# A grouped 1x1 convolution on one core: TensorE's unrolled program becomes a loop of 8 turns, and one ring becomes two

## The chip, the cores and the metric

The kernel runs on one NeuronCore of one Trainium2 chip. The metric is the device time of the whole program in microseconds (us); lower is better. The profile is of one execution on the chip.

## What is computed

The input x has 512 x 512 pixels of 192 channels, in bfloat16. The channels fall into 4 groups of 48, and each group is multiplied by its own 48 x 48 matrix. With k = 1 there is no padding, so it is one small matrix product per pixel and group:

```python
xg = x.reshape(1, 512, 512, 4, 48)
out = jnp.einsum('bhwgc,gcd->bhwgd', xg, w[0, 0])
return out.reshape(1, 512, 512, 192)
```

That is 262144 pixels of 384 B in and 384 B out, 201 MB in all.

## The kernel before

**Columns, groups, pairs, pieces.** The image is cut into pieces. A piece of `size` columns usually gives each of the 128 partitions of the on-chip memory `size` neighbouring pixels; a column is thus 128 pixels, one in each partition. Four columns are a *group*, two groups are a *pair*. `plan_pieces` lays the pieces out: a first slot in four small pieces (`HEAD`: 8, 20, 28 and 32 columns), then slots of `BIG` = 104 columns, and a last one of 48. There are 520 groups and 260 pairs.

**The ring.** All pieces live in one ring of 520 columns, five slots of 104. The results of a piece are written over its own input, and the piece is stored from there. So SyncE, which issues the loads (L217), waits in `wait_slot` until the piece five slots earlier has been stored. ScalarE issues the stores (L298).

**The work on a pair.** TensorE transposes the pair's pixels into `xT_ps` (L247, 12 transposes against an identity), VectorE copies them to one of three buffers `xT_sb` (L286, one copy a pair), TensorE multiplies them with block-shaped weights `wt` into `o_ps` (L262, 12 matmuls), and ScalarE copies each group's result from `o_ps` to the ring (L304, one copy a group). On TensorE the transposes of the next pair stand ahead of the matmuls of this one:

```python
for pair in range(NP):
    if pair + 1 < NP:
        transposes(pair + 1)
    matmuls(pair)
```

The semaphores `t_done`, `e_done`, `mm_done` and `fa_done` count pairs transposed, pairs copied by VectorE, groups multiplied and groups copied by ScalarE. All five engines' programs are written out in full: TensorE's has 3120 transposes, 3120 matmuls and as many weight loads.

**The shared piece.** One slot (`SHARED_AT`) is not spread over all 128 partitions. `SHARED` lists its blocks as (first row, rows, parts, columns, queue). A DMA whose outermost size is 4 is spread over four DMA engines, one whose outermost size is 11 over eleven. Before, two blocks of 16 rows and 72 columns go out in 4 parts from SyncE (and their stores from ScalarE), and one block of 44 rows and 64 columns in 11 parts from GpSimd. [...] Together the shares go to 15 of the 16 DMA engines; DMA engine 4 gets none.

**Stores at the end.** In the last slots (`LATE`) a piece is stored in two halves; a last piece of full size would be stored in four parts.

Of the kernel before, what the change touches and what calls it, by code (L numbers as in the profile page):

```python
# [12 lines left out]
UC = 2 * C  # L13
# [10 lines left out]

BIG = 104
RCOLS = 5 * BIG
HEAD = (8, 20, 28, 32)
LATE = 6
LATE_PARTS = (52, 52)
LAST_PARTS = (32, 32, 24, 16)  # L30
SHARED_AT = (9,)
SHARED_COLS = 72
SYNC, POOL = 0, 1
SHARED = ((0, 16, 4, SHARED_COLS, SYNC), (32, 16, 4, SHARED_COLS, SYNC), (52, 44, 11, 64, POOL))
CURSOR = 5
NXP = 4
NXS = 3
NOB = 4
# [21 lines left out]
class Piece:  # L60

    def __init__(self, i, slot, at, g0, size, shares, pix):
        self.i, self.slot, self.at, self.size = i, slot, at, size
        self.g0, self.g1 = g0, g0 + size // 4
        self.full = shares is None
        self.blocks = []
        for (r0, rows, parts, cols, queue) in shares or ((0, 128, 1, size, SYNC),):
            self.blocks.append(Block(r0, rows, parts, cols, queue, pix))
            pix += rows * cols
        self.pix_end = pix  # L70
        assert size % 4 == 0 and self.at + size <= RCOLS

# [4 lines left out]
def plan_pieces(npix):  # L77
    few = sum(rows * cols for _, rows, _, cols, _ in SHARED)
    at = list(SHARED_AT)
    if npix < len(at) * few + 128 * (sum(HEAD) + BIG * (at[-1] + 2)):  # L80
        at = []
    cols = (npix - few * len(at)) // 128
    assert cols % 4 == 0
    head = list(HEAD) if cols >= sum(HEAD) + BIG else []
    mid = cols - sum(head)
    slots = [[(BIG, None)]] * (mid // BIG) + ([[(mid % BIG, None)]] if mid % BIG else [])
    for i in at:
        slots.insert(i, [(SHARED_COLS, SHARED)])
    if head:
        slots.insert(0, [(s, None) for s in head])  # L90
    pieces, g, pix = [], 0, 0
    for n, parts in enumerate(slots):
        c = n * BIG % RCOLS
        for s, shares in parts:
            pieces.append(Piece(len(pieces), n, c, g, s, shares, pix))
            c, g, pix = c + s, pieces[-1].g1, pieces[-1].pix_end
    assert pix == npix
    return pieces


def bass_standalone__grouped__vision_kernel(nc, x, w, out):
# [7 lines left out]
    NG = pieces[-1].g1  # L109
    NP = (NG + 1) // 2  # L110

    xf = x.rearrange("b h w c -> (b h w) c")
# [17 lines left out]
    for p in pieces:  # L130
        late = pieces[-1].slot - p.slot
        parts = LAST_PARTS if late == 0 else LATE_PARTS if late < LATE else (BIG,)
        c = 0
        for n in parts if p.size == BIG and p.full else (p.size,):
            stores.append((p, c, c + n, p.g0 + (c + n) // 4))
            c += n
# [4 lines left out]
    with ExitStack() as es:  # L141
        block = es.enter_context(nc.Block())
        ring = es.enter_context(nc.sbuf_tensor("ring", [128, RCOLS * C], BF16))
        xT_sb = [es.enter_context(nc.sbuf_tensor(f"xT_sb{i}", [128, 4 * UC], BF16)) for i in range(NXS)]
# [14 lines left out]
        cur_sem = sem("cur_sem")  # L159
        cur = es.enter_context(nc.sbuf_tensor("cur", [CURSOR, 2 * len(pooled), 2, 32], BF16))  # L160
        w_sem, id_sem, e_sem, wb_sem, wc_sem = (sem(s) for s in ("w_sem", "id_sem", "e_sem", "wb_sem", "wc_sem"))
        p0_sem, p1_sem = sem("p0_sem"), sem("p1_sem")
        t_done, mm_done = sem("t_done"), sem("mm_done")
        e_done, fa_done = sem("e_done"), sem("fa_done")

        def columns(g):
            p = piece_of[g]
            at = p.at + 4 * (g - p.g0)
            return ring[:, at * C:(at + 4) * C]

        def wait_slot(wq, p):
            for q in pieces:
                if q.slot == p.slot - RCOLS // BIG:
                    wq.wait(st_sem[q.i], st_val[q])
                    if q in pl_sem:
                        wq.wait(ps_sem[q], pool_val[q])

        @block.gpsimd
        def _(gp):
# [12 lines left out]

            def pool_dmas(p, ap, inward, done):
                for dram, sbuf in transfers(ap, ring, p, POOL):
                    n = turns[0]
                    few = xf[0:CURSOR, 0:128].rearrange("p (a b) -> p a b", a=2)[:, :, 0:32]
                    gp.dma_start(cur[:, n], few).then_inc(cur_sem, 16)  # L197
                    turns[0] += 1
                    gp.dma_start(*((sbuf, dram) if inward else (dram, sbuf))).then_inc(done, 16)  # L199

            for p in pooled:
                wait_slot(wq, p)
                pool_dmas(p, xf, True, pl_sem[p])
                wq.wait(fa_done, p.g1)
                pool_dmas(p, of, False, ps_sem[p])
            for p in pooled:
# [3 lines left out]
        @block.sync  # L210
        def _(sp):
            wq = Waiter(sp)
            sp.dma_start(w_sb[:], wv).then_inc(w_sem, 16)  # L213
            for p in pieces:
                wait_slot(wq, p)
                for dram, sbuf in transfers(xf, ring, p, SYNC):
                    sp.dma_start(sbuf, dram).then_inc(ld_sem[p.i], 16)  # L217

        @block.tensor
        def _(pe):  # L220
            wq = Waiter(pe)

            def build_weights():
                wq.wait(e_sem, 1)
                wq.wait(w_sem, 16)
                last = None
# [6 lines left out]

            def transposes(pair):
                wq.wait(e_done, pair - 1)
                last = None
                for g in groups(pair):
                    p = piece_of[g]
                    if g == p.g0:
                        wq.wait(ld_sem[p.i], 16 * len(p.on(SYNC)))  # L240
                        if p in pl_sem:
                            wq.wait(pl_sem[p], pool_val[p])
                    xg = columns(g)
                    for ul in range(2):
                        for tc in range(3):
                            j = ul * 3 + tc
                            last = pe.transpose(xT_ps[:, g % NXP, j * 128:(j + 1) * 128],  # L247
                                                xg[:, j * 128:(j + 1) * 128], ident[:])
                last.then_inc(t_done, 1)

            def matmuls(pair):
                wq.wait(e_done, pair + 1)
                for g in groups(pair):
                    xs = xT_sb[pair % NXS][:, g % 2 * 2 * UC:(g % 2 + 1) * 2 * UC]
                    wq.wait(fa_done, g - 1)
                    last = None
                    for ul in range(2):
                        v = 2 * g + ul
                        for tc in range(3):
                            j = ul * 3 + tc  # L260
                            c0_, c1_ = COLR[tc]
                            last = pe.matmul(o_ps[:, v % NOB, c0_:c1_], lhsT=xs[:, j * 128:(j + 1) * 128],  # L262
                                             rhs=wt[:, WOFF[tc]:WOFF[tc] + (c1_ - c0_)],
                                             start=(tc == 0), stop=(tc == 2), skip_group_check=True)
                    last.then_inc(mm_done, 1)

            build_weights()
            wq.wait(id_sem, 1)
            transposes(0)
            wq.wait(wc_sem, 1)  # L270
            for pair in range(NP):
                if pair + 1 < NP:
                    transposes(pair + 1)
                matmuls(pair)

        @block.vector
        def _(dve):
# [3 lines left out]
            for pair in range(NP):  # L281
                n = len(groups(pair))
                b0 = pair * 2 % NXP
                wq.wait(t_done, pair + 1)
                wq.wait(mm_done, 2 * (pair - NXS + 1))
                dve.tensor_copy(xT_sb[pair % NXS][:, 0:n * 2 * UC].rearrange("p (g c) -> p g c", g=n),  # L286
                                xT_ps[:, b0:b0 + n, 0:2 * UC]).then_inc(e_done, 1)

        @block.scalar
        def _(act):  # L290
# [3 lines left out]
            def store():  # L294
                p, c0, c1, g1 = todo.pop(0)
                wq.wait(fa_done, g1)
                for dram, sbuf in transfers(of, ring, p, SYNC, c0, c1):
                    act.dma_start(dram, sbuf).then_inc(st_sem[p.i], 16)  # L298

            for g in range(NG):  # L300
                wq.wait(mm_done, g + 1)
                v = 2 * g
                dst = columns(g).rearrange("p (u c) -> p u c", u=2)
                act.copy(dst, o_ps[:, v % NOB:v % NOB + 2, 0:UC]).then_inc(fa_done, 1)  # L304
                while todo and todo[0][3] <= g:
                    store()
            while todo:
                store()
            for p in pieces:
# [29 lines left out]
```

## Time and profile before

| | us |
|---|---|
| median of 3 runs | 483.42 (482.58 to 484.23) |
| the profiled execution | 483.69 |
| its span, first to last instruction | 480.8 |
| around the span (the difference) | 2.9 |
| TensorE busy (matmuls and transposes) | 430.3 |
| ScalarE busy | 391.9 |
| VectorE busy | 249.6 |
| bytes moved by DMA, mean rate | 202.22 MB, 421 GB/s |

Read it with care for one thing: the share of an engine's busy time is a mean over the span, and a matmul's end is modelled, so a busy TensorE isn't one at its peak. The page has parts for busy time, the span in 40 slices, the DMA queues, the chain of work that ended last, the costliest groups of instructions and the DMA issues. Part 3 names the DMA queues by number: q1 carries SyncE's loads, q10 ScalarE's stores, q0 GpSimd's transfers, and q8 the code that TensorE runs. A group's row gives busy time and the mean duration of one instruction, then the engine's idle time ahead of them and what ended most of it. A row of the waits names who waited for whom, the total in us, how often, and the longest. The last compute instruction before begins near 460 us; the last store (2304 KB) is issued at 460.7 us and takes 19.7 us to land.

### The profile page before, as it was taken

What the parts mean: (1) busy time and instruction counts of PE and PEld (TensorE: products, weight loads), DVE (VectorE), ACT (ScalarE), POOL (GpSimd) and SP (SyncE); (2) the same over time, 40 slices, a digit from 0 to 9 for tenths busy, and PEclk for the clock granted to TensorE, in tenths of its full rate; (3) what the DMA queues carried; (4) which work ended last, traced back from release to release, by engine and by line L of the source; (5) the groups of instructions that cost most, each with busy time, mean ns of one, the idle gap of its engine ahead of it and who ended that gap; (6) DMA issues with size and microseconds to landing.
All of it is one profiled execution on the core that took longest, in us unless ns stands there. A gap on an engine that the chain in (4) does not pass through costs nothing.

```text
span 480.8 us, 13914 instructions
## 1 busy us (share of the span) xinstructions
PE 430.3 (89%) x6250; PEld 390.5 (81%) x6250; DVE 249.6 (52%) x261; ACT 391.9 (81%) x521; POOL 3.7 (1%) x12
## 2 busy tenths in 40 slices
PE   5979999999999999999679998989898999999910
PEld 5878898898898899889578887978787898898810
DVE  2535655655655655565335553545454556556500
ACT  2959999999998999899649995979797989999920
POOL 1000000000000001000000000000000000000000
PEclk9989999999999999999979998999999999999965
DMA  8999999999999999999999999999999999999995
GB/s 329 428 436 434 413 432 415 413 421 433 428 433 427 438 421 427 423 439 430 428 423 438 434 418 438 435 423 430 431 427 435 432 428 426 420 423 431 428 422 233
DMA packets 7913, 202.22 MB, mean 421 GB/s; under 512 B 1176, under 2 KB 1176, under 8 KB 1688
## 3 DMA queue, kind: packets, MB, share of 16 engines
q1 hardware_dynamic: 3560, 99.60, 48.5%
q10 hardware_dynamic: 4072, 99.58, 48.5%
q0 software_dynamic: 224, 2.16, 1.1%
q8 instruction: 49, 0.80, 0.6%
q14 instruction: 8, 0.07, 0.0%
HBM read 100.68 MB, written 100.66 MB: 419 GB/s over the span
## 4 chain that ended last, share of the span: by engine, by line
PE 47%; another core or an unknown queue 24%; DMA 23%; SPq 1%; issue 1%; ACT 0%
PE o_ps L262 27%; PE xT_ps L247 20%; DMA ring<-in_x_dram 13%; DMA out_dram<-ring 10%; SPq L217 1%; ACT ring L304 0%; SPq L213 0%; SPq L51 0%
## 5 line engine op out<-in xcount | busy, mean ns | idle before, releaser
L304 ACT CAST ring<-o_ps 128x768 bf16<-128x768 f32 x520 | 390.6, 802 | 68.0 <-PE o_ps L262 57.4
L286 DVE COPY xT_sb<-xT_ps 128x1536 bf16<-128x1536 bf16 x260 | 249.0, 958 | 205.1 <-PE xT_ps L247 205.1
L262 PE MATMUL o_ps<-wt,xT_sb 128*128 128x144 bf16 (+1 forms) x3120 | 290.6, 235 | 5.7 <-ACT ring L304 1.8
L262 PEld LDWEIGHTS o_ps<-wt,xT_sb 128*128 128x128 bf16 x3120 | 210.8, 98 | 43.1 <-ACT ring L304 32.8
L247 PE MATMUL xT_ps<-ident,ring 128*128 128x128 bf16 x3120 | 221.6, 222 | 20.9 <-DMA ring<-in_x_dram 20.5
L247 PEld LDWEIGHTS xT_ps<-ident,ring 128*128 128x128 bf16 x3120 | 190.8, 99 | 23.1 <-DMA ring<-in_x_dram 20.1
L197 POOL DMA_DIRECT2D cur<-in_x_dram x2 | 1.2, 622 | 242.7 <-DMA out_dram<-ring 188.8
L230 PE MATMUL o_ps<-w_sb,esel 48*128 48x48 bf16 x10 | 0.6, 209 | 2.8 <-DMA w_sb<-in_w_dram 2.8
L230 PEld LDWEIGHTS o_ps<-w_sb,esel 48*128 48x128 bf16 x10 | 0.4, 111 | 2.8 <-issue 2.8
L280 DVE CAST wt<-o_ps 128x480 bf16<-128x480 f32 x1 | 0.7, 658 | 3.4 <-PE o_ps L230 3.4
L304 ACT ACT_TABLE_LOAD x1 | 1.3, 1283 | 0.8 <-PEq L324 0.8
L199 POOL DMA_DIRECT2D ring<-in_x_dram x1 | 0.6, 563 | 0.0
L199 POOL DMA_DIRECT2D out_dram<-ring x1 | 0.6, 559 | 0.0
L184 POOL TENSOR_SCALAR_AFFINE_SELECT esel<-esel 48x272 bf16<-48x272 bf16 x1 | 0.4, 402 | 0.0
L181 POOL MEMSET esel<- 48x272 bf16 x1 | 0.3, 317 | 0.3 <-POOLq L324 0.3
L188 POOL TENSOR_SCALAR_AFFINE_SELECT ident<-ident 128x128 bf16<-128x128 bf16 x1 | 0.3, 282 | 0.0
L182 POOL MEMSET ident<- 128x128 bf16 x1 | 0.2, 198 | 0.0
L324 POOL MEMSET const-bfloat16-1.0<- 128x1 bf16 x1 | 0.1, 101 | 0.0
L324 POOL MEMSET const-uint8-127<- 128x1 uint8 x1 | 0.1, 101 | 0.0
L324 POOL MEMSET const-float32-0.0<- 128x1 f32 x1 | 0.1, 98 | 0.3 <-issue 0.3
L324 POOL MEMSET const-float32-1.0<- 128x1 f32 x1 | 0.1, 98 | 0.0
## 6 DMA issues: line engine op xcount, KB each, us to landing
ring<-in_x_dram SPq DMA_DIRECT2D x18, 4992.0 KB, 33.4
out_dram<-ring ACTq DMA_DIRECT2D x13, 4992.0 KB, 51.4
out_dram<-ring ACTq DMA_DIRECT2D x10, 2496.0 KB, 43.5
ring<-in_x_dram SPq DMA_DIRECT2D x1, 2304.0 KB, 16.3
out_dram<-ring ACTq DMA_DIRECT2D x1, 2304.0 KB, 19.7
ring<-in_x_dram SPq DMA_DIRECT2D x1, 1536.0 KB, 11.1
out_dram<-ring ACTq DMA_DIRECT2D x1, 1536.0 KB, 40.8
ring<-in_x_dram SPq DMA_DIRECT2D x1, 1344.0 KB, 7.9
```

What stands on the lines that cost most here:

```text
L181: gp.memset(esel[:], 1.0).then_inc(p0_sem, 1)
L184: gp.affine_select(out=esel[:], in_=esel[:], pattern=[[-1, ECOLS]], compare_op=AluOpType.is_equal, fill=0.0, base=ESHIFT, channel_multipli ...
L197: gp.dma_start(cur[:, n], few).then_inc(cur_sem, 16)
L199: gp.dma_start(*((sbuf, dram) if inward else (dram, sbuf))).then_inc(done, 16)
L217: sp.dma_start(sbuf, dram).then_inc(ld_sem[p.i], 16)
L230: last = pe.matmul(o_ps[:, NOB - 1, col:col + CG], lhsT=esel[:, s0:s0 + 128], rhs=w_sb[:, g, :], start=True, stop=True, skip_group_check=True)
L247: last = pe.transpose(xT_ps[:, g % NXP, j * 128:(j + 1) * 128], xg[:, j * 128:(j + 1) * 128], ident[:])
L262: last = pe.matmul(o_ps[:, v % NOB, c0_:c1_], lhsT=xs[:, j * 128:(j + 1) * 128], rhs=wt[:, WOFF[tc]:WOFF[tc] + (c1_ - c0_)], start=(tc == ...
L280: dve.tensor_copy(wt[:], o_ps[:, NOB - 1, 0:WCOLS]).then_inc(wc_sem, 1)
L286: dve.tensor_copy(xT_sb[pair % NXS][:, 0:n * 2 * UC].rearrange("p (g c) -> p g c", g=n), xT_ps[:, b0:b0 + n, 0:2 * UC]).then_inc(e_done, 1)
L304: act.copy(dst, o_ps[:, v % NOB:v % NOB + 2, 0:UC]).then_inc(fa_done, 1)
L324: nc = _bacc.Bacc("TRN2", target_bir_lowering=False, num_devices=1)
```

## The change

- **Loop.** TensorE's program is one pair of transposes, then a loop of 8 turns (`pe.Fori`). A turn does 32 pairs, 64 groups (`LOOP`), and at its end subtracts what the turn used from three semaphores, so that each turn can wait for the same constants. The matmuls of the last group stand behind the loop.
- **Two rings.** `xin` and `xout` have 256 columns each, three slots of 88, 84 and 84. A loop turn goes round them once. A load waits for the transposes (`t_done`) of the pieces that lay there before; ScalarE waits for the store of what lay in `xout` before it writes.
- **Landings through GpSimd.** TensorE no longer waits for a piece's own load semaphore. GpSimd waits for each load in turn and adds the piece's pairs to `ready`; TensorE waits for `ready` at the places in a turn where some piece begins (`starts`).
- **Shared piece.** Now 32 rows in 4 parts from SyncE and 88 rows in 11 parts from GpSimd, all of 64 columns: 120 rows, 8 for each of 15 DMA engines. It stands in slot 12, with a piece of 24 columns behind it in the same slot. In all there are 513 groups.
- **Buffers and waits.** `xT_sb` has two buffers instead of three, and some waits that the order on TensorE implies are gone. A store is issued one group later, without a wait for ScalarE's own copy.
- **Stores at the end.** The pieces of the last slots go out in halves, the last full one in parts of 24, 20, 20 and 20, and the last piece has 4 columns.

The diff, cut to its core:

```diff
-BIG = 104
-RCOLS = 5 * BIG
+RING = 256
+SLOTS = (88, 84, 84)
 HEAD = (8, 20, 28, 32)
 LATE = 6
-LATE_PARTS = (52, 52)
-LAST_PARTS = (32, 32, 24, 16)
-SHARED_AT = (9,)
-SHARED_COLS = 72
+LAST_PARTS = (24, 20, 20, 20)
+LOOP = RING // 4
+SHARED_AT = (12,)
+SHARED_COLS = 64
 SYNC, POOL = 0, 1
-SHARED = ((0, 16, 4, SHARED_COLS, SYNC), (32, 16, 4, SHARED_COLS, SYNC), (52, 44, 11, 64, POOL))
+SHARED = ((0, 32, 4, 64, SYNC), (32, 88, 11, 64, POOL))
 CURSOR = 5
 NXP = 4
-NXS = 3
+NXS = 2
 NOB = 4
...
-    pieces, g, pix = [], 0, 0
-    for n, parts in enumerate(slots):
-        c = n * BIG % RCOLS
+    pieces, g, pix, n = [], 0, 0, 0
+    while cols:
+        size = SLOTS[n % len(SLOTS)]
+        c = sum(SLOTS[:n % len(SLOTS)])
+        parts = [(s, None) for s in HEAD] if n == 0 and cols >= size else []
+        if n in at:
+            parts = [(SHARED_COLS, SHARED)]
+        left = size - sum(s for s, _ in parts)
+        if min(left, cols):
+            parts.append((min(left, cols), None))
         for s, shares in parts:
             pieces.append(Piece(len(pieces), n, c, g, s, shares, pix))
+            cols -= 0 if shares else s
             c, g, pix = c + s, pieces[-1].g1, pieces[-1].pix_end
+        n += 1
     assert pix == npix
     return pieces
...
+    LP = LOOP // 2
+    turns_of_loop = max(NP - 1, 0) // LP
+    starts = sorted({p.g0 // 2 % LP for p in pieces})
...
-        parts = LAST_PARTS if late == 0 else LATE_PARTS if late < LATE else (BIG,)
+        half = p.size // 8 * 4
+        parts = (p.size,)
+        if p.full and p.size in SLOTS and late < LATE:
+            parts = LAST_PARTS if late == 1 and p.size == sum(LAST_PARTS) else (p.size - half, half)
         c = 0
-        for n in parts if p.size == BIG and p.full else (p.size,):
+        for n in parts:
...
-        ring = es.enter_context(nc.sbuf_tensor("ring", [128, RCOLS * C], BF16))
+        xin = es.enter_context(nc.sbuf_tensor("xin", [128, RING * C], BF16))
+        xout = es.enter_context(nc.sbuf_tensor("xout", [128, RING * C], BF16))
...
-        def columns(g):
-            p = piece_of[g]
-            at = p.at + 4 * (g - p.g0)
-            return ring[:, at * C:(at + 4) * C]
-
-        def wait_slot(wq, p):
-            for q in pieces:
-                if q.slot == p.slot - RCOLS // BIG:
-                    wq.wait(st_sem[q.i], st_val[q])
-                    if q in pl_sem:
-                        wq.wait(ps_sem[q], pool_val[q])
+        ready, e_left, o_left = sem("ready"), sem("e_left"), sem("o_left")
+
+        def columns(ring, g):
+            c = g % LOOP * 4
+            return ring[:, c * C:(c + 4) * C]
+
+        def before(p):
+            return [q for q in pieces if q.g0 < p.g0 - LOOP + p.size // 4 and q.g1 > p.g0 - LOOP]
...
-            for p in pooled:
-                wait_slot(wq, p)
-                pool_dmas(p, xf, True, pl_sem[p])
-                wq.wait(fa_done, p.g1)
-                pool_dmas(p, of, False, ps_sem[p])
+            for p in pieces:
+                ahead = pieces[p.i + 1] if p.i + 1 < len(pieces) else None
+                if ahead in pooled:
+                    wq.wait(t_done, max([(q.g1 + 1) // 2 for q in before(ahead)], default=0))
+                    pool_dmas(ahead, xf, xin, True, pl_sem[ahead])
+                wq.wait(ld_sem[p.i], 16 * len(p.on(SYNC)))
+                if p in pooled:
+                    wq.wait(pl_sem[p], pool_val[p])
+                pairs = (NP if p is pieces[-1] else p.g1 // 2) - p.g0 // 2
+                if pairs:
+                    gp.sem_inc(ready, pairs)
+                if p.i and pieces[p.i - 1] in pooled:
+                    q = pieces[p.i - 1]
+                    wq.wait(mm_done, q.g1 + 2)
+                    pool_dmas(q, of, xout, False, ps_sem[q])
...
-                wait_slot(wq, p)
-                for dram, sbuf in transfers(xf, ring, p, SYNC):
+                wq.wait(t_done, max([(q.g1 + 1) // 2 for q in before(p)], default=0))
+                for dram, sbuf in transfers(xf, xin, p, SYNC):
                     sp.dma_start(sbuf, dram).then_inc(ld_sem[p.i], 16)
...
-            def transposes(pair):
-                wq.wait(e_done, pair - 1)
+            def transposes(j, gs):
+                if j % LP in starts:
+                    n = min((s - j) % LP or LP for s in starts)
+                    pe.wait_ge(ready, min(j + n, NP - first[0]))
...
-                for g in groups(pair):
-                    p = piece_of[g]
-                    if g == p.g0:
-                        wq.wait(ld_sem[p.i], 16 * len(p.on(SYNC)))
-                        if p in pl_sem:
-                            wq.wait(pl_sem[p], pool_val[p])
-                    xg = columns(g)
+                for g in gs:
+                    xg = columns(xin, g)
...
-            def matmuls(pair):
-                wq.wait(e_done, pair + 1)
-                for g in groups(pair):
-                    xs = xT_sb[pair % NXS][:, g % 2 * 2 * UC:(g % 2 + 1) * 2 * UC]
-                    wq.wait(fa_done, g - 1)
+            def matmuls(j, gs):
+                pe.wait_ge(e_left, j + 1)
+                for g in gs:
+                    xs = xT_sb[j % NXS][:, g % 2 * 2 * UC:(g % 2 + 1) * 2 * UC]
+                    pe.wait_ge(o_left, g + 1)
...
+            first = [0]
             build_weights()
-            wq.wait(id_sem, 1)
-            transposes(0)
-            wq.wait(wc_sem, 1)
-            for pair in range(NP):
-                if pair + 1 < NP:
-                    transposes(pair + 1)
-                matmuls(pair)
+            pe.wait_ge(id_sem, 1)
+            pe.sem_inc(o_left, 2)
+            transposes(0, groups(0))
+            pe.wait_ge(wc_sem, 1)
+            if turns_of_loop:
+                with pe.Fori(0, turns_of_loop):
+                    for j in range(LP):
+                        transposes(j + 1, range(2 * j + 2, 2 * j + 4))
+                        matmuls(j, range(2 * j, 2 * j + 2))
+                    pe.sem_inc(ready, -LP)
+                    pe.sem_inc(e_left, -LP)
+                    pe.sem_inc(o_left, -LOOP)
+            first[0] = LP * turns_of_loop
+            for j in range(NP - first[0]):
+                g0 = 2 * first[0]
+                if j + 1 < NP - first[0]:
+                    transposes(j + 1, [g - g0 for g in groups(first[0] + j + 1)])
+                matmuls(j, [g - g0 for g in groups(first[0] + j)])
...
-                wq.wait(mm_done, 2 * (pair - NXS + 1))
                 dve.tensor_copy(xT_sb[pair % NXS][:, 0:n * 2 * UC].rearrange("p (g c) -> p g c", g=n),
-                                xT_ps[:, b0:b0 + n, 0:2 * UC]).then_inc(e_done, 1)
+                                xT_ps[:, b0:b0 + n, 0:2 * UC]).then_inc(e_left, 1)
...
-                wq.wait(fa_done, g1)
-                for dram, sbuf in transfers(of, ring, p, SYNC, c0, c1):
+                for dram, sbuf in transfers(of, xout, p, SYNC, c0, c1):
                     act.dma_start(dram, sbuf).then_inc(st_sem[p.i], 16)
...
             for g in range(NG):
+                p = piece_of[g]
+                if g == p.g0:
+                    for q in before(p):
+                        wq.wait(st_sem[q.i], st_val[q])
+                        if q in pooled:
+                            wq.wait(ps_sem[q], pool_val[q])
...
-                dst = columns(g).rearrange("p (u c) -> p u c", u=2)
-                act.copy(dst, o_ps[:, v % NOB:v % NOB + 2, 0:UC]).then_inc(fa_done, 1)
-                while todo and todo[0][3] <= g:
+                dst = columns(xout, g).rearrange("p (u c) -> p u c", u=2)
+                act.copy(dst, o_ps[:, v % NOB:v % NOB + 2, 0:UC]).then_inc(o_left, 1)
+                while todo and todo[0][3] < g:
                     store()
             while todo:
+                act.wait_ge(o_left, todo[0][3] - LOOP * turns_of_loop + 2)
                 store()
```

More of the change, by code (lines that the diff above doesn't have):

```diff
@@ L70, in __init__ @@
         self.pix_end = pix
-        assert size % 4 == 0 and self.at + size <= RCOLS
+        assert size % 4 == 0 and self.at + size <= RING
     def on(self, queue):
@@ L79, in plan_pieces @@
     at = list(SHARED_AT)
-    if npix < len(at) * few + 128 * (sum(HEAD) + BIG * (at[-1] + 2)):
+    if npix < len(at) * few + 128 * RING * (2 + at[-1] // len(SLOTS)):
         at = []
@@ L83, in plan_pieces @@
     assert cols % 4 == 0
[L84 to L90, printed above, removed]
-    pieces, g, pix = [], 0, 0
-    for n, parts in enumerate(slots):
-        c = n * BIG % RCOLS
+    pieces, g, pix, n = [], 0, 0, 0
[8 more added lines that the diff above has]
+            parts.append((min(left, cols), None))
         for s, shares in parts:
             pieces.append(Piece(len(pieces), n, c, g, s, shares, pix))
+            cols -= 0 if shares else s
             c, g, pix = c + s, pieces[-1].g1, pieces[-1].pix_end
+        n += 1
     assert pix == npix
@@ L159, in bass_standalone__grouped__vision_kernel @@
         cur_sem = sem("cur_sem")
-        cur = es.enter_context(nc.sbuf_tensor("cur", [CURSOR, 2 * len(pooled), 2, 32], BF16))
+        cur = es.enter_context(nc.sbuf_tensor("cur", [CURSOR, 2 * max(len(pooled), 1), 2, 32], BF16))
         w_sem, id_sem, e_sem, wb_sem, wc_sem = (sem(s) for s in ("w_sem", "id_sem", "e_sem", "wb_sem", "wc_sem"))
@@ L163, in bass_standalone__grouped__vision_kernel @@
         t_done, mm_done = sem("t_done"), sem("mm_done")
-        e_done, fa_done = sem("e_done"), sem("fa_done")
-        def columns(g):
-            p = piece_of[g]
-            at = p.at + 4 * (g - p.g0)
-            return ring[:, at * C:(at + 4) * C]
-        def wait_slot(wq, p):
-            for q in pieces:
-                if q.slot == p.slot - RCOLS // BIG:
-                    wq.wait(st_sem[q.i], st_val[q])
-                    if q in pl_sem:
-                        wq.wait(ps_sem[q], pool_val[q])
+        ready, e_left, o_left = sem("ready"), sem("e_left"), sem("o_left")
[4 more added lines that the diff above has]
+            return [q for q in pieces if q.g0 < p.g0 - LOOP + p.size // 4 and q.g1 > p.g0 - LOOP]
         @block.gpsimd
@@ L191, in _, with pool_dmas @@
             turns = [0]
-            def pool_dmas(p, ap, inward, done):
+            def pool_dmas(p, ap, ring, inward, done):
                 for dram, sbuf in transfers(ap, ring, p, POOL):
@@ L220, in _ @@
         def _(pe):
-            wq = Waiter(pe)
             def build_weights():
-                wq.wait(e_sem, 1)
-                wq.wait(w_sem, 16)
+                pe.wait_ge(e_sem, 1)
+                pe.wait_ge(w_sem, 16)
                 last = None
@@ L232, in build_weights @@
                 last.then_inc(wb_sem, 1)
-            def transposes(pair):
-                wq.wait(e_done, pair - 1)
+            def transposes(j, gs):
+                if j % LP in starts:
+                    n = min((s - j) % LP or LP for s in starts)
+                    pe.wait_ge(ready, min(j + n, NP - first[0]))
                 last = None
-                for g in groups(pair):
-                    p = piece_of[g]
-                    if g == p.g0:
-                        wq.wait(ld_sem[p.i], 16 * len(p.on(SYNC)))
-                        if p in pl_sem:
-                            wq.wait(pl_sem[p], pool_val[p])
-                    xg = columns(g)
+                for g in gs:
+                    xg = columns(xin, g)
                     for ul in range(2):
                         for tc in range(3):
-                            j = ul * 3 + tc
-                            last = pe.transpose(xT_ps[:, g % NXP, j * 128:(j + 1) * 128],
-                                                xg[:, j * 128:(j + 1) * 128], ident[:])
+                            i = ul * 3 + tc
+                            last = pe.transpose(xT_ps[:, g % NXP, i * 128:(i + 1) * 128],
+                                                xg[:, i * 128:(i + 1) * 128], ident[:])
                 last.then_inc(t_done, 1)
-            def matmuls(pair):
-                wq.wait(e_done, pair + 1)
-                for g in groups(pair):
-                    xs = xT_sb[pair % NXS][:, g % 2 * 2 * UC:(g % 2 + 1) * 2 * UC]
-                    wq.wait(fa_done, g - 1)
+            def matmuls(j, gs):
[3 more added lines that the diff above has]
+                    pe.wait_ge(o_left, g + 1)
                     last = None
@@ L259, in matmuls @@
                         for tc in range(3):
-                            j = ul * 3 + tc
+                            i = ul * 3 + tc
                             c0_, c1_ = COLR[tc]
-                            last = pe.matmul(o_ps[:, v % NOB, c0_:c1_], lhsT=xs[:, j * 128:(j + 1) * 128],
+                            last = pe.matmul(o_ps[:, v % NOB, c0_:c1_], lhsT=xs[:, i * 128:(i + 1) * 128],
                                              rhs=wt[:, WOFF[tc]:WOFF[tc] + (c1_ - c0_)],
```

## The prediction

> **What bounds the kernel now.** I read the page's slices first, then its DMA queues, then busy time by stretches of the span (short ones at the end), then the waits.
>
> The page, parts 1 and 2 (busy time of each engine; the forty slices):
>
> ```profile
> PE 430.3 (89%) x6250; PEld 390.5 (81%) x6250; DVE 249.6 (52%) x261; ACT 391.9 (81%) x521; POOL 3.7 (1%) x12
> ...
> DMA  8999999999999999999999999999999999999995
> GB/s 329 428 436 434 413 432 415 413 421 433 428 433 427 438 421 427 423 439 430 428 423 438 434 418 438 435 423 430 431 427 435 432 428 426 420 423 431 428 422 233
> ```
>
> TensorE looks fuller than ScalarE, but only the DMA row is at 9 from the second slice to the last but one. The page's part 3 says what fills it:
>
> ```profile
> q1 hardware_dynamic: 3560, 99.60, 48.5%
> q10 hardware_dynamic: 4072, 99.58, 48.5%
> q0 software_dynamic: 224, 2.16, 1.1%
> q8 instruction: 49, 0.80, 0.6%
> ```
>
> Loads, stores, GpSimd's transfers and TensorE's code together are 98.7% of what 16 DMA engines had in the span. The stretches (us, then busy us and count by engine, granted clock, DMA share, GB/s) show where the rest is:
>
> ```profile
> 444.00:456.00 12.00, 11.85 (x178) 10.69 (x176) 7.24 (x8) 10.94 (x16) 0.00 (x0) 1.00 1.01 427
> 456.00:468.00 12.00, 3.19 (x42) 2.51 (x40) 1.38 (x2) 4.38 (x6) 0.00 (x0) 0.72 1.00 430
> 468.00:472.00 4.00, 0.00 (x0) 0.00 (x0) 0.00 (x0) 0.00 (x0) 0.00 (x0) 0.50 0.84 361
> 472.00:476.00 4.00, 0.00 (x0) 0.00 (x0) 0.00 (x0) 0.00 (x0) 0.00 (x0) 0.50 0.79 339
> 476.00:480.80 4.80, 0.00 (x0) 0.00 (x0) 0.00 (x0) 0.00 (x0) 0.00 (x0) 0.50 0.14 61
> ```
>
> No engine computes after 461 us; the end is DMA alone. The share falls in steps: at 0.79 of 16, about three DMA engines have finished, the others near 476, and a few run to 480. So the time is the longest of sixteen nearly full DMA engines. Compute only has to keep them fed, and does:
>
> ```profile
> ACT ring L304 <- PE o_ps L262: 57.4, 119, 7.2
> ...
> PEld o_ps L262 <- ACT ring L304: 32.8, 142, 1.5
> PE xT_ps L247 <- DMA ring<-in_x_dram: 20.5, 9, 5.7
> ```
>
> TensorE waits for loads nine times, and ScalarE then for TensorE. Between such waits ScalarE's copies set the pace:
>
> ```profile
> L304 ACT CAST ring<-o_ps 128x768 bf16<-128x768 f32 x520 | 390.6, 802 | 68.0 <-PE o_ps L262 57.4
> ```
>
> In the timeline at 160 us five copies take 4.07 us, 0.815 us a group.
>
> **Sixteen chains.** The trace lists every DMA packet with start and duration. Under load a packet starts 3 ns before another ends, so the packets can be strung into 16 chains, one per DMA engine. A load packet of 39936 B takes 1.476 us (27.06 B/ns), one of 27648 B 1.025 us, one of 24576 B 0.912 us. The shared pieces' packets label the chains:
> - Four carry 16 packets of 27648 B (16.4 us), the SYNC share. They end at 476.9, 477.3, 480.0 and 480.0.
> - Eight carry 8 of 24576 B (7.3 us), the POOL share, and all code pages between them, six or seven each. They end at 475.8 to 477.7, mean 476.5.
> - Three carry the POOL share and no pages: 468.0 to 468.7, mean 468.4. So six pages cost 8.1 us, some 1.3 us each: a page packet takes 1.0 us and the data packet behind it about 1.85 instead of 1.476.
> - One carries neither, yet ends at 476.2: its store packets take about 1.58 us all through. It is DMA engine 4, left out now as after.
>
> **The change, part by part.**
>
> *Shares.* A shared piece holds 7680 pixels instead of 5120, so whole rows give each DMA engine (262144-7680)/16 = 15904 pixels, 160 fewer. A pixel is 768 B in and out, so that is 123 KB, 4.5 us less for all sixteen. The share becomes 8 rows of 64 columns in and out, 16 packets of 0.912 us, 14.6 us, for all but engine 4.
>
> *Code.* The loop body is 768 matmuls with their weight loads plus 37 waits, semaphore steps and the branch: 1573 instructions, 6.1 pages of 256; TensorE's whole program is 6.4 pages where it was 49.9. If the body stays in TensorE's instruction store, pages fall from 49 to at most 7. No trace here has a backward branch, so the bounds are 0 and 49 pages saved, or even some lost. I take saved: successive pages go to the eight DMA engines in a fixed turn, every eighth to the same one, which looks like eight slots, and 6.1 pages plus one ahead fit in eight. Against it: the first page is fetched at 16.1 us, when 281 instructions have run, so a page is asked for as soon as one is left; if that overwrites the page just left, the loop's head is gone before the first branch back.
>
> [...]
>
> *Sum by chain,* with the body held:
> - SYNC four: -4.5-16.4+14.6 = -6.3, so 470.6 to 473.7.
> - Eight with pages: -4.5-7.3+14.6-8.1 = -5.3, mean 471.2.
> - Three without: -4.5-7.3+14.6 = +2.8, mean 471.2.
> - Engine 4: -4.5, 471.7.
>
> The last chain ends at 473.7. From the last packet to the span's end were 0.8 us (480.8-480.0), from span to the profiled execution's time 2.9 (483.69-480.8): 477.4 us. That execution stands 0.27 us over the median of 483.42. The seven first pages fall on chains with 2.5 us to spare.
>
> *Branches back.* Seven are taken. Each costs TensorE three semaphore steps, an addition and the branch; at the 0.24 us of the shortest waits in the timeline, about a microsecond, 7 us in all, hidden as below. With a missing page: 1.0 us for the page, up to two packets of 1.476 ahead of it, 4 us.
>
> *Ring.* 520 columns shared in place become 256 in and 256 out. A load now waits for the transposes of the slot three back, not for a store five slots back (before, SP waited 342.9 us in 15 waits for stores). ScalarE waits for the store three slots back, and behind it on ScalarE are only later copies and their stores. A column is 49152 B each way, 0.114 us at 430 GB/s, so a slot of 84 costs DMA 19.2 us and compute 21 x 0.815 = 17.1. Compute is the faster, so when it frees a slot the DMA still has work: cost nothing. If that cover goes, a refill starts on an empty queue; the smallest load (384 KB, 0.9 us of transfer) landed in 3.3, so 2.4 us are lost each time. There are 513 groups instead of 520, 5.7 us less for ScalarE, so compute needs 418 us. At the start 256 columns keep the DMA busy until about 31 us; the first slot of 22 groups is through by about 26 (ScalarE did 20 copies in the first 24 us): no gap, but the margin is small.
>
> *GpSimd* now passes each landing on to TensorE by `ready`. Queued behind its waits are its own two shared transfers; the pooled store waits for two further groups of a six-group piece, so the next slot's `ready` is not late. A relay is priced at the 0.3 us that GpSimd's first wait in the waits' view lasts, at most 37 of them, 11 us of compute spread over the span; but the next loads are queued by then, so the DMA loses nothing.
>
> *Smaller edits.* Two xT_sb buffers, dropped waits that the order of TensorE implies, stores issued one group later, a tail in parts down to 4 columns: nothing, since DMA has a backlog to the end.
>
> **The rivals.**
>
> *Code is fetched again each turn (slower).* Then 8 turns of 7 pages are 56, seven on each of the eight chains: 471.2+9.3 = 480.5, plus 0.8 and 2.9 is 484.2. Stalls of 4 us are covered by three slots a turn at 19.2-17.1 = 2.1 us each, 6.3, with little left, so I add 0 to 6 us: 484 to 490, middle 487. If pages past the loop's end come in as well and are thrown away, up to eight a turn, 9 us more: 496. It decides from the point where the body and what is fetched ahead exceed the store. For it speaks the eager first fetch, against it the turn of eight. [...] Chance 0.22.
>
> *The smaller ring starves the DMA (about level).* Two or three empty starts of 2.4 us at the beginning and at branches undo the gain: 480 to 485. The 33 us in which a load now lands (in the median) speak for it; the 2.1 us of compute in hand per slot against. Chance 0.10.
>
> *The rotation stops but the longest chain doesn't shorten (the change doesn't do what it says).* If the SYNC share is not on the four chains I think, the last chain stays at 480 less 4.5, 479 us in all. The landing of each share four by four speaks against. Chance 0.05, inside the range.
>
> **Numbers.** Body held: 0.63, 475 to 480, likeliest 477.4. Chains as long as now but for the 4.5 us: 0.05, 479. Refetch 0.22, 487. Starved 0.10, 482.5, of it 0.02 faster, 0.05 the same, 0.03 slower. A measurement of this kernel can tell 0.3%, 1.5 us. So faster 0.70, same 0.05, slower 0.25. The range goes from 474.5 (all chains level at 471, less a microsecond) to 488.5, past the middle of the refetch case.
>
> **What would show it.** Held: queue q8 with about 7 packets, DMA share near 1.00 until 470, then a fall within 3 us. Refetched: 56 packets or more, TensorE waiting some 4 us every 64 groups, and a DMA tail with seven or eight engines late. Starved: DMA slices under 9 in mid-span. The prediction is wrong if q8 stays above 49 packets, or if any mid-span slice falls below 400 GB/s.

## The result, and the profile after

| | before | after |
|---|---|---|
| median, four runs each on one chip, us | 483.81 (482.58 to 484.23) | 488.89 (488.58 to 489.35) |
| profiled execution, us | 483.69 | 489.35 |
| its span, us | 480.8 | 487.6 |

The changed kernel takes 1.0117 times as long (95% interval 1.0102 to 1.0132): 5.1 us slower by the medians (5.7 by the ratio), where the prediction had 6.0 us faster.

The forty slices and the queues of the page of after:

```profile
DMA  8999999999999999999999999999999999999976
GB/s 310 432 411 434 429 433 421 431 429 431 431 439 432 431 432 434 400 331 388 434 429 442 405 392 428 414 418 437 426 427 429 436 428 437 427 428 423 430 293 269
...
q1 hardware_dynamic: 4276, 98.52, 47.9%
q10 hardware_dynamic: 5076, 98.50, 47.5%
q0 software_dynamic: 352, 4.33, 2.6%
q8 instruction: 6, 0.10, 0.1%
```

Three things are to be seen.

**The code stays.** q8 has 6 packets where it had 49. They come at 19.3, 28.5, 38.2, 45.7, 54.6 and 61.8 us, all in the first of eight turns (the second begins at 64.3 us).

**The DMA engines are busy and move less.** The DMA row stands at 9 through the middle of the span, yet the row under it falls to 331 and 388 GB/s in the slices from 207 to 232 us, and again to 392 near 286. Those are the load and the store of the shared piece. Two stretches of after (us, then busy us and count by engine, granted clock, DMA share, GB/s) show it closer:

```profile
204.00:216.00 12.00, 11.89 (x182) 10.93 (x180) 6.70 (x7) 10.99 (x15) 0.00 (x0) 1.00 0.99 340
216.00:228.00 12.00, 8.90 (x113) 8.26 (x111) 4.27 (x5) 6.95 (x11) 0.00 (x0) 0.86 1.03 357
```

The share is 0.99 and more at 340 to 357 GB/s, where before moved 427 in a full stretch. The busy share alone doesn't tell this loss; bytes have to be read beside it. In the packet list, packets of 24576 B, 0.912 us each before, now take 1.153 us in the mean on GpSimd's queue (the longest 2.644), 1.207 among SyncE's loads and 1.022 among the stores of the same rows.

**The end is ragged.** Stretches of the end of after:

```profile
464.00:468.00 4.00, 3.92 (x59) 3.43 (x57) 2.65 (x3) 3.68 (x6) 0.00 (x0) 1.00 0.44 187
...
472.00:476.00 4.00, 3.96 (x61) 3.59 (x59) 2.53 (x3) 3.52 (x6) 0.00 (x0) 1.00 0.79 328
476.00:480.00 4.00, 3.96 (x64) 3.67 (x62) 2.25 (x3) 3.73 (x6) 0.00 (x0) 1.00 0.58 236
480.00:484.00 4.00, 1.75 (x21) 1.15 (x18) 0.56 (x1) 2.86 (x4) 0.00 (x0) 1.00 0.79 328
484.00:487.60 3.60, 0.00 (x0) 0.00 (x0) 0.00 (x0) 0.00 (x0) 0.00 (x0) 0.77 0.55 215
```

Before, no engine computed after 461 us and the DMA emptied a backlog. After, TensorE and ScalarE are busy until about 482 and 483 us, and the DMA engines stand partly idle (0.44, 0.58) waiting for results to store. The last load landed at 448.6 us. Two rows of the waits of after say what had made compute late:

```profile
PEld o_ps L272 <- ACT xout L330: 52.7, 126, 12.6
...
ACT xout L330 <- DMA out_dram<-xout: 44.6, 14, 12.2
```

ScalarE waited 44.6 us in 14 waits for a slot of `xout` to be stored, and TensorE for ScalarE behind it. No such wait is in the profile of before.

### The profile page after: what moved, and what is told of

Same layout as the page of the kernel before. It is cut to its first block, busy times and chain, and to the rows that moved or that the text cites. A ratio compares the mean times of both kernels' runs of the same rounds, so it can differ in the third digit from the quotient of the medians.

```text
span 487.6 us, 13577 instructions
## 1 busy us (share of the span) xinstructions
PE 428.0 (88%) x6172; PEld 387.5 (79%) x6172; DVE 246.3 (51%) x258; ACT 387.0 (79%) x514; POOL 3.7 (1%) x12
## 3 DMA queue, kind: packets, MB, share of 16 engines
q0 software_dynamic: 352, 4.33, 2.6%
## 4 chain that ended last, share of the span: by engine, by line
DMA 68%; PE 29%; ACT 1%; issue 1%; SPq 0%; ACTq 0%; POOLq 0%
DMA out_dram<-xout 67%; PE o_ps L272 17%; PE xT_ps L257 12%; DMA xin<-in_x_dram 2%; ACT xout L330 1%; SPq L231 0%; SPq L227 0%; ACTq L51 0%; POOLq L215 0%
## 5 line engine op out<-in xcount | busy, mean ns | idle before, releaser
L330 ACT CAST xout<-o_ps 128x768 bf16<-128x768 f32 x513 | 385.7, 801 | 95.2 <-DMA out_dram<-xout 44.6
L307 DVE COPY xT_sb<-xT_ps 128x1536 bf16<-128x1536 bf16 x257 | 245.6, 956 | 231.1 <-PE xT_ps L257 231.1
L257 PE MATMUL xT_ps<-ident,xin 128*128 128x128 bf16 x3084 | 219.1, 222 | 6.1 <-POOLq L215 4.4
L257 PEld LDWEIGHTS xT_ps<-ident,xin 128*128 128x128 bf16 x3084 | 188.6, 99 | 8.0 <-POOLq L215 5.2
## 6 DMA issues: line engine op xcount, KB each, us to landing
xin<-in_x_dram SPq DMA_DIRECT2D x16, 4032.0 KB, 28.5
```

The source lines that it names most:

```text
L257: last = pe.transpose(xT_ps[:, g % NXP, i * 128:(i + 1) * 128], xg[:, i * 128:(i + 1) * 128], ident[:])
L330: act.copy(dst, o_ps[:, v % NOB:v % NOB + 2, 0:UC]).then_inc(o_left, 1)
```

## The experiments

After the result there were two theories. **Layout** (P in what was expected): the shared piece's new rows make its packets slow, and through late stores ScalarE too. **Rings** (R): three slots a ring have too little slack, whatever the share does. The loop was undone too, to see what it brings.

Wherever an edit puts the share on other rows, the number of pixels for each DMA engine is meant to stay that of the kernel it starts from, unless it says otherwise. The diffs are cut to the lines that matter.

### After, with each share on other rows

```diff
-SHARED = ((0, 32, 4, 64, SYNC), (32, 88, 11, 64, POOL))
+SHARED = ((0, 16, 4, 64, SYNC), (32, 16, 4, 64, SYNC),
+          (52, 44, 11, 64, POOL), (20, 12, 3, 64, POOL), (96, 32, 8, 64, POOL))
...
```

Every part has four rows now, in two blocks from SyncE and three from GpSimd. GpSimd's tiny transfer over five rows (`cur`) is left out ahead of the block of eight parts. Loop, rings and slots are those of after.

> [...] Theory P (the share's rows lie in blocks of other DMA engines, and packets are stretched there): the rate in the slices from 195 to 232 us comes back from 331-400 GB/s to about 430, the shared packets of 24576 B take 0.912 us, ScalarE's waits for stores (44.6 us) shrink since no DMA engine lags, and the time falls from 488.9 to 476-480 us. Theory R (the three-slot output ring makes ScalarE wait for stores and compute late, whatever the share does): the slices heal but ScalarE still waits over 35 us for stores and the time stays at 484 us or above.

Measured: 480.84 us, 0.9945 of before (0.9929 to 0.9962), so 8.05 us less than after (by the two ratios, 1.0117 - 0.9945, 8.3 us) and just above the 476 to 480 that the layout theory gave. The same stretches and GpSimd's queue in its profile:

```profile
204.00:216.00 12.00, 11.86 (x180) 10.78 (x177) 6.85 (x8) 11.14 (x15) 0.00 (x0) 1.00 1.00 427
216.00:228.00 12.00, 11.85 (x178) 10.69 (x176) 7.34 (x8) 10.93 (x16) 0.00 (x0) 1.00 0.99 423
```

```profile
q0 software_dynamic: 608, 4.33, 2.1%
```

The hole of 340 and 357 GB/s is gone. The same 4.33 MB take 2.1% of the DMA engines' span instead of 2.6%, and all 240 packets of 24576 B take 0.912 us. ScalarE's wait for stores halves:

```profile
ACT xout L332 <- DMA out_dram<-xout: 21.4, 6, 5.6
```

So the layout (rows and blocks together) cost 8.05 us, more than the whole loss. Half of ScalarE's wait remains, which layout does not explain.

### Before, with the share of after

```diff
-SHARED_COLS = 72
+SHARED_COLS = 64
-SHARED = ((0, 16, 4, SHARED_COLS, SYNC), (32, 16, 4, SHARED_COLS, SYNC), (52, 44, 11, 64, POOL))
+SHARED = ((0, 32, 4, 64, SYNC), (32, 88, 11, 64, POOL))
```

One ring, no loop: only the share is that of after.

> The kernel before with the shared piece of the kernel after (32 rows in 4 parts, 88 rows in 11, 64 columns), its ring and unrolled program as they were. Theory P: packets are stretched here too, the slices in which the share is loaded and stored fall below 410 GB/s, and the time rises by 5 to 9 us, to 489-493 us. Theory R: no stretch without the small rings; by the chains the eight DMA engines with code pages then end last, at 476.5-4.5-7.3+14.6 = 479.3 us, so 483 us, the same as before.

Measured: 492.1 us, 1.0165 of before (1.0136 to 1.0195), 8.8 us slower by the medians and 8.0 by the ratio (its four runs lie between 490.06 and 493.25). Its slices:

```profile
DMA  8999999999999999999999999999999999999994
GB/s 329 454 431 397 446 431 409 411 425 427 435 427 434 423 443 425 391 372 438 430 423 402 355 395 395 421 424 437 425 411 440 422 424 430 426 418 429 427 404 171
```

Again two holes (372, then 355 to 395) under a row of nines. GpSimd's packets of 24576 B take 1.204 us in the mean, the longest 4.329. The loss needs neither loop nor rings.

### After's loop undone

```diff
-    turns_of_loop = max(NP - 1, 0) // LP
+    turns_of_loop = 0
```

The kernel with other rows, its TensorE program written out again.

> As e1_own_rows, but TensorE's loop written out in full (no backward branch, 49 pages of code fetched again). It prices the loop alone. If the pages cost what the chains said (8.1 us on each of eight DMA engines, with 1 to 2.5 us to spare), the time is 5 to 7 us above e1_own_rows. If code pages are hidden beside the data, or the loop's branches cost as much, the two are within 1 us.

Measured: 486.41 us, 1.0057 of before (1.0041 to 1.0074), 5.57 us more than with the loop. Its part 3 has the code back:

```profile
q8 instruction: 49, 0.80, 0.6%
```

The loop is worth 5.57 us. The unrolled kernel is still 3 us slower than before, though its share's packets are at 0.912 to 0.917 us: something else in the change costs time. ScalarE's wait for stores, which before doesn't have, may be a part of it:

```profile
ACT xout L332 <- DMA out_dram<-xout: 30.8, 9, 6.7
...
PE xT_ps L259 <- POOLq L217: 13.0, 4, 10.0
```

The second row is TensorE's wait for GpSimd's relay, which the sixth experiment takes up.

### Before, with GpSimd's share one step of four rows on

```diff
-SHARED = (..., (52, 44, 11, 64, POOL))
+SHARED = (..., (56, 44, 11, 64, POOL))
```

Rows 56 to 99 in place of 52 to 95, in as many parts and from the same queue.

> [...] Theory P: packets are stretched while the share runs (the 24576 B packets take more than 0.912 us), half as many of them as in the kernel after, and the time rises by 1 to 4 us. Rival (it is the volume on GpSimd's queue, 88 rows instead of 44, or eight rows for each DMA engine, that stretches packets): packets stay at 0.912 us and the time at 483-484 us.

Measured: 483.76 us, 1.0012 of before (1.0002 to 1.0021; ten runs). The packets stretched as the layout theory wants, from 0.912 us to a mean of 1.022 with the longest at 1.853, but the time rose by only 0.4 us, where 1 to 4 were expected. Blocks, sizes and places in DRAM are those of before, so the rows alone stretch packets here; but so small a stretch cost little. A packet of 24576 B takes 0.912 us and one of 39936 B 1.476: 8.5 ns, and 27.2 B/ns. Counting what loads, stores and GpSimd's transfers take beyond that, a DMA engine loses 6.2 us in the mean here, against 4.9 before and 12.2 with the share of after.

### Four slots a ring

```diff
-SLOTS = (88, 84, 84)
-HEAD = (8, 20, 28, 32)
+SLOTS = (64, 64, 64, 64)
+HEAD = (8, 12, 16, 28)
-LAST_PARTS = (24, 20, 20, 20)
+LAST_PARTS = (16, 16, 16, 16)
-SHARED_AT = (12,)
+SHARED_AT = (16,)
```

The kernel with other rows and the loop. The rings keep 256 columns each.

> e1_own_rows with both rings cut in four slots of 64 columns instead of 88, 84 and 84, so that a slot is handed back sooner. Theory R2 (what is left over the predicted sum, 480.8 against 477.4 us, is compute held back by whole slots waiting for their stores, so that TensorE ends late and the DMA runs dry at the end): ScalarE's waits for stores fall from 21.4 us to under 10, the DMA share between 464 us and the end rises, and the time falls to 477-479.5 us. Rival (it is GpSimd's relay of the landings, or the many smaller transfers): 480-483 us.

Measured: 476.49 us, 0.9858 of before (0.9842 to 0.9875), the fastest here: 4.35 us less than with three slots, and a little below the 477 to 479.5 expected. Its end:

```profile
456.00:464.00 8.00, 3.24 (x44) 2.56 (x41) 1.51 (x2) 4.14 (x6) 0.00 (x0) 0.83 1.02 432
464.00:468.00 4.00, 0.00 (x0) 0.00 (x0) 0.00 (x0) 0.00 (x0) 0.00 (x0) 0.50 0.99 413
468.00:472.00 4.00, 0.00 (x0) 0.00 (x0) 0.00 (x0) 0.00 (x0) 0.00 (x0) 0.50 0.93 384
472.00:474.90 2.90, 0.00 (x0) 0.00 (x0) 0.00 (x0) 0.00 (x0) 0.00 (x0) 0.50 0.18 70
```

This is the end that the prediction described: compute done near 460 us, full DMA to 468, a fall within 3 us. ScalarE's wait for stores is down once more, though not under the 10 us expected:

```profile
ACT xout L332 <- DMA out_dram<-xout: 14.8, 8, 4.0
```

The likely reason is that a finer slot comes free in smaller steps, so that less has to land before ScalarE may go on. The edit also changes the first pieces, the last parts and the shared piece's place; how much each of these gave was not taken apart.

### Unrolled, without GpSimd's relay

```diff
-                pe.wait_ge(ready, min(j + n, NP - first[0]))
...
+                    if g == p.g0:
+                        pe.wait_ge(ld_sem[p.i], 16 * len(p.on(SYNC)))
+                        if p in pooled:
+                            pe.wait_ge(pl_sem[p], pool_val[p])
```

The unrolled kernel of the third experiment, with TensorE waiting for the loads themselves.

> e3_own_rows_unrolled, but TensorE waits for each piece's own load semaphores, not for GpSimd's count. It prices the relay alone. If relaying delays the DMA's refills, the time falls from 486.4 by 1 us or more; if the DMA's chains and the rings set the end, it stays within 0.7 us.

Measured: 485.94 us, 1.0050 of before (1.0033 to 1.0067), 0.5 us less than with the relay, within the two ranges (485.10 to 486.90 and 485.75 to 486.95). TensorE's wait has changed its name and hardly its size:

```profile
PE xT_ps L261 <- DMA xin<-in_x_dram: 12.6, 3, 9.9
```

So TensorE's wait is mostly for landings that had not come yet, and the relay is not the cause of the unrolled kernel's loss.

### Before, with the larger share on the other rows

```diff
-SHARED_COLS = 72
+SHARED_COLS = 64
-SHARED = ((0, 16, 4, SHARED_COLS, SYNC), (32, 16, 4, SHARED_COLS, SYNC), (52, 44, 11, 64, POOL))
+SHARED = ((0, 16, 4, 64, SYNC), (32, 16, 4, 64, SYNC),
+          (52, 44, 11, 64, POOL), (20, 12, 3, 64, POOL), (96, 32, 8, 64, POOL))
```

> The kernel before (one ring of 520 columns in place, unrolled program, three xT_sb buffers) with the shared piece of e1_own_rows. Against e3_own_rows_unrolled it differs in the rings, the relay and the buffers alone. By the chains the eight DMA engines with code pages end last, at 479.3 us, so 483 us. If the two rings of 256 columns cost what e3 (486.4) lies above its own chains, this kernel is at 482-484 us; if the chains' sum is what was off by 3.4 us, it is at 486-487 us too.

Measured: 483.76 us, 1.0008 of before (0.9996 to 1.0021; ten runs). The larger share alone changes nothing that can be told. The kernel stands beside two others: it differs from the one with after's share only in rows and blocks and is 8.3 us faster (7.6 by the ratios); and it differs from the unrolled kernel with two rings in the rings and what came with them, and is 2.65 us faster.

## Why the prediction was wrong

From before to after in four steps, each the difference of two medians above:

| step | us |
|---|---|
| share of 120 rows, on the rows of the first experiment (before to the last experiment) | +0.3 |
| two rings of three slots, with what came along (to the unrolled kernel) | +2.65 |
| loop of 8 turns (to the first experiment) | -5.57 |
| shares on the rows that the change gives them (to after) | +8.05 |
| sum | +5.5 |

Each step starts where the one ahead of it ends, so the sum is the direct difference by construction (+5.5 beside the runs of before taken with the last experiments, 483.43; +5.1 beside those taken with after). It doesn't show that the steps are independent: in another order they may have other sizes.

The packets show what three of the steps, and the four slots, are made of. The span of a profiled run is what its packets take on a DMA engine, in the mean over 16, plus what that DMA engine stands idle. The bytes are the same in all these kernels. Differences in us, rounded:

| step | 8.5 ns for each packet | stretch beyond that and 27.2 B/ns | code | idle | span |
|---|---|---|---|---|---|
| two rings of three slots | +0.9 | +0.8 | 0.0 | +1.0 | +2.8 |
| loop of 8 turns | 0.0 | -1.8 | -2.6 | -1.4 | -5.8 |
| shares on the rows of the change | -0.1 | +5.6 | 0.0 | +3.0 | +8.4 |
| four slots instead of three | +1.1 | -2.0 | 0.0 | -3.4 | -4.3 |

**Code: right.** The body was held, seven pages or fewer were forecast and six came. The forecast was -8.1 us on eight of sixteen chains, a mean of 4.05 us. Over all packets, a DMA engine's busy time falls from 477.6 to 473.2 us in the mean when the unrolled kernel gets the loop, 4.4 us, and the time by 5.57. That TensorE's store holds eight pages, as the forecast read from the turn of eight, no run shows: they show that a body of 6.1 pages stayed, with six fetches in all, after and in the first experiment.

**Branches back: right.** The forecast was a microsecond each, hidden. The timeline of after shows half of that ahead of the weight load at a turn's head:

```profile
120.59 0.67 PEld L257 LDWEIGHTS xT_ps<-ident,xin 128*128 128x128 bf16 x12 [0.48 <-issue]
```

**Shares: this step failed.** The sum had "16 packets of 0.912 us, 14.6 us". It took a packet's duration from before and assumed that it goes with size alone. Counting the stretch as above, each DMA engine lost 10.6 us in the mean after, 5.0 with the other rows and 4.9 before: 5.6 us per DMA engine that no term held. It comes at the share's load and store: between 192 and 304 us the stretch is 6.8 us after and 0.7 with the other rows, and with one ring 7.1 and 0.6. The other 3.0 us between the two spans are DMA engines standing idle. The likely road to them is stores that land late behind such packets: ScalarE waits 23.2 us more for them (44.6 against 21.4), and its last copy ends at 483.0 us instead of 473.6.

The clue lay in the diff: the blocks of before start at rows 0, 32 and 52, those of the change at 0 and 32, with 8 rows in a line to a part. That the layout of the share costs this time is shown by two pairs of kernels with the same 7680 pixels in the share, by the author's count as many for each DMA engine: 8.05 us apart with the loop, 8.3 without. Each pair differs in the number of blocks too (two against five). The shift by four rows left the blocks alone and stretched packets, and five blocks on the other rows did not, so the stretch comes from the rows; what the blocks add to the 8 us was not measured alone. *Why* rows decide was not shown. The trace names neither a packet's rows nor its DMA engine, so that the slow rows lie in blocks of other DMA engines (theory P) stays the author's conjecture, and the number 4 of the DMA engine without a share is the author's count. What was measured is the pattern: packets of 24576 B take 0.912 us with the blocks of before and 0.912 to 0.917 us with the five blocks of the first and third experiments, and in the mean 1.02 to 1.21 us in the three layouts of after, of the second and of the fourth.

**Ring: a mis-sized term.** "Cost nothing" rested on a compute of 17.1 us for a slot against 19.2 of DMA. Two rings of three slots, with what came along, cost 2.65 us, and slots of 64 give 4.35 back. The prediction named the queue behind a store that ScalarE waits for, and then priced only the DMA's idle time, not the compute that is put off past the last load. In the unrolled kernel with two rings ScalarE waits 30.8 us for stores, where before only SyncE and GpSimd did; one of these waits is 6.7 us long, more than the mean margin of 2.1 us a slot. Yet late compute can be only a part of the 2.65 us. By the second table idle DMA engines make up 1.0 us; 0.9 us is the 9968 packets in place of 8240 that smaller pieces make, and 0.8 us is stretch whose cause the runs don't show. What the finer slots give back is mostly idle time. Of the two rings, the two `xT_sb` buffers, the other piece sizes and the relay, only the relay was taken out alone.

**The end.** The forecast span was 474.5 us (473.7 + 0.8). With other rows it was 479.2, with four slots too 474.9. So the sum by chain fits a kernel whose compute keeps ahead and whose packets run nearly at full rate; the change is not that kernel. That it fits within 0.4 us is partly luck, since the four slots also have 1.1 us more for the number of packets and 2.0 us less stretch.

**The rivals.** Refetched code did not come, though 487 us was near the measured time: the right number by the wrong road. The starved ring (480 to 485) was partly real, but what starved was the end, and mid-span slices never fell under 9. The prediction's own sign, a mid-span slice below 400 GB/s, did show: 331, 388 and 392. No rival had the moved rows slow the packets. The measured 488.89 us stands 0.4 us above the forecast's range, whose top was put there for the refetched code. The range's lower end is a slip: chains level at 471 us and a microsecond less give 473.7 us, not 474.5.

## What to carry to other kernels

When a DMA bound kernel moves a transfer that only some of the DMA engines carry to other rows, price it as a possible change of rate, not of bytes alone: here packets of 24576 B took 0.912 us on some rows and 1.02 to 1.21 us in the mean on others, and the two layouts of the share were 8.05 us apart. The runs give no rule for which rows are slow, so compare the durations of the packets on the old rows and the new. Read GB/s beside the DMA's busy share, since a slowed packet counts as busy: a share of 0.99 was 340 GB/s after, one of 1.00 was 427 with the other rows. Where a ring seems too small, try cutting it finer first: here four slots of 64 columns beat three of 88, 84 and 84 in the same 256, by 4.35 us.

## What the runs showed of the hardware

- TensorE kept a loop of 1573 instructions, 6.1 pages of 256: after, six page fetches in the first turn, none in the seven after it, and 0.48 us ahead of the weight load at a turn's head.
- A packet of 24576 B beside full traffic took 0.91 to 0.92 us in the mean on some rows and 1.02 to 1.21 us on others, up to 4.33; with 240 such packets on the others, in two blocks where there were five, the kernel with the loop is 8.05 us slower.
- A shift of one block by four rows, with a mean of 1.022 us on 88 packets, cost 0.4 us; 240 packets with means of 1.03 to 1.20 in the same ring cost 8.3.
- The loop takes 49 code pages down to 6: with the same rings, 4.4 us less busy time for a DMA engine in the mean and 5.57 us less time.
